# A fused retention and feed-forward kernel: one unit more transposed by DMA, half a group more by seven products, and a new order of all instructions

## The chip, the cores and the metric

One core of one Trainium2 chip. Engines: TensorE (PE, matrix products), VectorE (DVE), ScalarE (ACT), GpSimd (POOL, here only an issuer of DMAs) and SyncE (SP, another issuer of DMAs). The metric is device time in microseconds; of several runs the median is used.

## The reference

```python
scores = q @ k^T / sqrt(64)                       # 8 batches, 8 heads, 576 positions, head dim 64
ret    = scores * gamma[h] ** (i - j) for i >= j, else 0
attn   = ret @ v
x      = attn, heads side by side                 # 4608 tokens x 512
h      = x @ w_in                                 # 512 x 2048
out    = max(0.01 h, h) @ w_out                   # 2048 x 512, float32
```

## The kernel before

The tokens are cut into 36 units of 128 (each two chunks of 64) and 9 groups of 512 tokens (four units). A unit `u` goes through these jobs:

- `ld{u}.1`, `.0`, `.2`: load k, q, v (a DMA from SP or POOL; the pool holds four units).
- `ck`, `cq`, `cv`: cast k, scale q and v to half precision (one DVE instruction, or on ACT eight scalings, one for each head, for q and v).
- `tp{u}.1`, `.0` on TensorE and the copies `yt{u}.1`, `.0`: the transposed k and q. From unit `CFG["turned"]` on, one DMA transpose `tr{u}` on SP's queue does that instead.
- `sb` (state sums, TensorE), `st`, `sg` (running state, DVE), `sx` (its cast).
- `ca` (the state's part of the output and the scores, TensorE), `mk` (mask, DVE), `ow` (own chunk's part, TensorE), `x{u}` (the result into `xT`).

Layer one of group 0 and group 1 is plain: jobs `h{g}.{f}.{t}` of 8 or 16 products on TensorE, followed by the activation `l...` on ACT (L643). The groups from 2 on take layer one by a scheme of seven products for four quadrants (Strassen's in Winograd's form): `a{g}.{n}.p1` to `.p7`, four matmuls of 256 columns each, on sums of inputs `xs` (DVE) and of weights `ws` (DVE), with copies `cA`, `u2`, `k5` out of the accumulators and the sums `12` and `22` on DVE. Layer two of each group is done the same way: `b{g}.p1` to `.p7`, each in two parts of eight matmuls, with input mixes `m` and weight mixes `wm` on DVE. `wi{f}` loads a quarter of `w_in` (two DMAs of POOL that convert to half precision), `wo{c}` a quarter of `w_out`, `so` stores.

A word `+7@0` is seven matmuls on a tile of zeros into accumulator 0, whose result nobody reads (`filler`, L957).

The order of all jobs is written out by hand as a list of words, `ORDER`, and each engine runs its own jobs in that order, one after the other; `@n` names the accumulator a job takes. The table `ENGINE` says which of DVE and ACT does a job that either can do. A job that waits holds up every later one on its engine.

## Time and profile before

| | |
|---|---|
| time, median of 3 runs | 283.44 us (283.22 to 283.71) |
| the profiled execution's own time | 285.72 us |
| its span | 283.9 us |
| PE busy | 273.8 us (96%) |
| DVE, ACT busy | 237.9 us (84%), 198.2 us (70%) |
| mean granted clock of TensorE | 0.982 |

Times in the profile are those of one execution, counted from the start of its span. A busy TensorE is not one at its peak, since its records overlap; so the length of a row of products, or the time from one job to the next, says what a product costs. The time that is idle on an engine counts only where the chain that ended last runs through it.

### The profile page before, as it was taken

The numbers are of one execution on the slowest core, as the hardware profiler recorded it, in microseconds if no ns is written. First come the engines' busy times: TensorE is split into PE (matmuls) and PEld (weight loads), VectorE is DVE, ScalarE is ACT, GpSimd is POOL, SyncE is SP. The second block draws the span as 40 slices with busy tenths as digits, with TensorE's granted clock in tenths as the row PEclk, the third lists the DMA queues.
The fourth block names the chain that finished last, engine by engine and source line by source line (L and its number), as shares of the span: only waits on it lengthen the run. The fifth ranks groups of instructions, "written<-read, shape, count | busy, mean of one in ns | idle before, by whom it ended". The sixth has DMA issues, their size and how long they took to land.

```text
span 283.9 us, 10247 instructions
## 1 busy us (share of the span) xinstructions
PE 273.8 (96%) x4411; PEld 232.3 (82%) x4411; DVE 237.9 (84%) x453; ACT 198.2 (70%) x434; POOL 40.9 (14%) x54
## 2 busy tenths in 40 slices
PE   7759999999999999999999999999999999999994
PEld 3539888888888888888888888888888888888883
DVE  2964568999998999889999999998899998975851
ACT  2233687676767997699859877898598975815840
POOL 8957795300000000000000000000000000000000
PEclk9956999999999999999999999999999999999999
DMA  7999999987898884699959479999499062002103
GB/s 224 274 195 213 220 262 249 299 204 177 235 178 196 198 215 95 171 225 231 194 130 251 91 208 186 239 171 242 106 248 210 6 183 76 3 2 105 45 18 130
DMA packets 114062, 49.00 MB, mean 173 GB/s; under 512 B 102689, under 2 KB 107425, under 8 KB 114017
## 3 DMA queue, kind: packets, MB, share of 16 engines
q1 hardware_dynamic: 106592, 34.87, 53.8%
q0 software_dynamic: 7136, 13.37, 19.7%
q8 instruction: 34, 0.56, 0.8%
q10 hardware_dynamic: 288, 0.11, 0.1%
q14 instruction: 12, 0.09, 0.1%
HBM read 36.81 MB, written 9.44 MB: 163 GB/s over the span
## 4 chain that ended last, share of the span: by engine, by line
PE 92%; DMA 4%; POOL 2%; DVE 1%; issue 0%; POOLq 0%
PE acc L898 40%; PE acc L822 31%; PE acc L636 11%; PE ot L540 5%; DMA t<-in_v_dram 4%; PE sc L443 2%; PE sc L434 2%; POOL t L344 2%; PE acc L400 1%; PE acc L957 0%; DVE osb L935 0%; DVE v L366 0%; DVE s L449 0%; POOLq L344 0%; POOLq L1009 0%
## 5 line engine op out<-in xcount | busy, mean ns | idle before, releaser
L898 PEld LDWEIGHTS <-gt 128*128 128x128 f16 x720 | 69.0, 98 | 8.7 <-issue 0.2
L898 PE MATMUL acc<-w_out,gt 128*128 128x256 f16 x432 | 54.4, 273 | 0.0
L822 PEld LDWEIGHTS <-w_in 128*128 128x128 f16 x448 | 43.1, 98 | 5.7 <-issue 0.3
L840 ACT ACTIVATE gt<-acc 128x512 f16<-128x512 f32 x56 | 33.4, 599 | 10.8 <-PE acc L822 10.6
L898 PE MATMUL acc<-w_mix,gt 128*128 128x256 f16 x288 | 36.2, 273 | 0.0
L822 PEld LDWEIGHTS <-w_sum 128*128 128x128 f16 x336 | 32.3, 98 | 4.2
L848 ACT ACTIVATE gt<-sum 128x512 f16<-128x512 f32 x56 | 33.9, 632 | 2.2 <-DVE sum L844 2.1
L822 PE MATMUL acc<-xT,w_in 128*128 128x256 f16 x224 | 33.1, 273 | 0.0
L822 PE MATMUL acc<-xs,w_sum 128*128 128x256 f16 x224 | 32.8, 273 | 0.0
L822 PE MATMUL acc<-xs,w_in 128*128 128x256 f16 x224 | 32.5, 273 | 0.0
L636 PE MATMUL acc<-xT,w_in 128*128 128x256 f16 (+1 forms) x320 | 32.2, 262 | 0.0
L449 DVE TENSOR_TENSOR s<-sc,cs 128x512 f16<-128x512 f32 x36 | 24.7, 686 | 8.3 <-PE sc L434 7.6
L898 PEld LDWEIGHTS <-mix 128*128 128x128 f16 x288 | 27.7, 98 | 3.3
L636 PEld LDWEIGHTS <-w_in 128*128 128x128 f16 x320 | 27.1, 104 | 2.5 <-DVE xT L589 0.2
L761 ACT COPY acc<-acc 128x512 f32<-128x512 f32 x32 | 18.4, 574 | 13.3 <-PE acc L822 9.1
L643 ACT ACTIVATE gt<-acc 128x512 f16<-128x512 f32 x32 | 17.9, 600 | 12.2 <-PE acc L636 12.1
L844 DVE TENSOR_TENSOR sum<-acc,u 128x512 f32<-128x512 f32 x28 | 19.1, 687 | 3.3 <-PE acc L822 1.9
L772 ACT COPY u<-acc 128x512 f32<-128x512 f32 x26 | 15.3, 589 | 8.9 <-PE acc L898 4.5
L366 DVE TENSOR_TENSOR qk<-t,cs 128x512 f16<-128x512 f32 x29 | 19.8, 685 | 1.9 <-DMA t<-in_q_dram 1.9
L844 DVE TENSOR_TENSOR sum<-acc,k 128x512 f32<-128x512 f32 x28 | 19.2, 686 | 2.3 <-PE acc L822 2.0
L366 DVE TENSOR_TENSOR v<-t,cs 128x512 f16<-128x512 f32 x29 | 19.7, 685 | 1.6 <-DMA t<-in_v_dram 1.5
L589 ACT CAST xT<-ot 128x512 f16<-128x512 f32 x28 | 16.3, 588 | 6.7 <-PE ot L540 6.4
(64 smaller groups left out, 453.8 us busy)
## 6 DMA issues: line engine op xcount, KB each, us to landing
out_dram<-osb SPq DMA_DIRECT2D x17, 512.0 KB, 4.3
t<-in_k_dram SPq DMA_DIRECT2D x22, 256.0 KB, 3.9
t<-in_q_dram SPq DMA_DIRECT2D x22, 256.0 KB, 3.8
t<-in_v_dram SPq DMA_DIRECT2D x20, 256.0 KB, 4.3
t<-in_v_dram POOLq DMA_DIRECT2D x12, 256.0 KB, 7.2
t<-in_q_dram POOLq DMA_DIRECT2D x10, 256.0 KB, 7.6
t<-in_k_dram POOLq DMA_DIRECT2D x10, 256.0 KB, 6.8
w_in<-in_moe_w_in_dram POOLq DMA_DIRECT2D x8, 256.0 KB, 7.8
```

The costliest lines, as they stand in the source:

```text
L366: engine[e].tensor_tensor(out=out, in0=t32[u, 2 * x][:], in1=decay(u, x), op=MUL)
L449: landed[u] = nc.vector.tensor_tensor(out=s[:], in0=sc[:, :, 0], in1=mask_sb.unsqueeze(1).unsqueeze(1).to_broadcast([P, 2, NP, CH]), op=MUL,)
L589: copies[xe](out=x_of(u).rearrange("q c (j t) -> q j c t", j=2), in_=at)
L636: nc.tensor.matmul(out=a[:, n, :], lhsT=w_in16[:, c, (f0 + n) * P : (f0 + n + 1) * P], rhs=x[:, c, t0 : t0 + nt], start=(n == 0 and c == 0 ...
L643: nc.scalar.activation(out=y[:, f0 : f0 + nf, t0 : t0 + nt], in_=a[:], func=mybir.ActivationFunctionType.Lrelu)
L761: copies[ce](out=B[:], in_=A[:])
L772: op("u2", ue, lambda: copies[ue](out=u2[:], in_=B[:]), [done["6"]], [u2], [B])
L822: nc.tensor.matmul(out=r[:, f, :], lhsT=w[:, c, (2 * n + f) * P : (2 * n + f + 1) * P], rhs=rhs[:, c, :], start=fresh and c == 0 and f == ...
L840: w = op(what, "ACT", lambda: nc.scalar.activation(out=to(), in_=r[:], func=lr), after, [y], [r])
L844: what, "DVE", lambda: nc.vector.tensor_tensor(out=s[:], in0=r[:], in1=plus[:], op=ADD),
L848: f"l{g}.{n}.{what}", "ACT", lambda: nc.scalar.activation(out=to(), in_=s[:], func=lr), [j], [y],
L898: nc.tensor.matmul(out=(r[tb] if isinstance(r, tuple) else r)[:, tb, :], lhsT=lhs[n]()[:, f, tb * P : (tb + 1) * P], rhs=rhs[n][:, f, :], ...
```

## The change

Three settings change and all orders are made anew:

- `turned` from 12 to 11: unit 11 is transposed by DMA (`tr11`) and not on TensorE (`tp11`, `yt11`).
- `half` from 0 to 1: in group 1, the plain jobs of half of the hidden columns (`h1.4`, `h1.6`, `h1.12`, `h1.14`) are replaced by two sets of seven products, `a1.2` and `a1.3`, with their sums of inputs `xs1`.
- `ORDER` and `ENGINE` are another list: there are 39 zero matmuls in place of 27, in lots of 13, 2, 4, 6, 7, 3, 1 and 3 ahead of the first layer-one job.

The helper for loading `w_in` can also load eighths now, which is unused (`halved` is empty).

```diff
-    turned=12,
-    half=0,
+    turned=11,
+    half=1,
+    halved=(),
...
 ORDER = """
-    ld0.1 ld0.0 ld1.0 ld0.2 ld1.1 ld1.2 ck0 +6@0 +1@1 +1@2 tp0.1@3 ld2.1 yt0.1 ld2.0 cq1 cq0 +7@0 tp1.0@1 ld3.1 yt1.0
...
+    ld0.1 ld0.0 ld1.0 ld1.1 ld0.2 ld1.2 ld2.2 ld2.1 cq0 cq1 ck0 ld3.2 +13@0 +2@1 tp0.0@2 ck1 tp0.1@3 ld2.0 cv0 yt0.1
...
+    tp3.0@3 ck3 sx2 cv3 +1@1 tp3.1@2 yt3.0 yt2.0 sb3 x0 cq4 ca2 tp4.0@1 st3.0 mk2 ld5.2 yt3.1 +3@3 ow2 st3.1 ld5.1
+    h0.0.0@0 sg3.1 x2 ck4 ld5.0 h0.0.128@3 sx3 yt4.0 ca3 l0.0.128 tp4.1@2 mk3 h0.0.256@1 wi2 ld6.1 h0.4.256@3
...
-        w_in_job[f] = add(f"wi{f}", "POOL", run)
+        j = add(f"wi{f}" + ("" if i is None else "ab"[i]), "POOL", run)
+        for e in (0, 1) if i is None else (i,):
+            w_in_job[2 * f + e] = j
...
-                after = [w_in_job[0], w_in_job[1], w_in_job[2], w_in_job[3]]
+                after = list(dict.fromkeys(w_in_job[f] for f in range(8)))
```

The engines' rows at three places. First POOL's DMA queue from its tenth load on, before (the names end with the tensor loaded; `x2` are two halves):

```order
L344 DMA t_1_216<-in_k_dram 64x8x64 x2
L344 DMA t_2_250<-in_v_dram 128x8x64
L612 DMA w_in_113<-in_moe_w_in_dram 64x4x512 x4
L344 DMA t_0_350<-in_q_dram 64x8x64 x2
L344 DMA t_2_363<-in_v_dram 64x8x64 x2
L612 DMA w_in_113<-in_moe_w_in_dram 64x4x512 x2
```

and after the change:

```order
L346 DMA t_0_229<-in_q_dram 64x8x64 x2
L346 DMA t_1_270<-in_k_dram 128x8x64
L614 DMA w_in_113<-in_moe_w_in_dram 64x4x512 x2
L346 DMA t_1_314<-in_k_dram 64x8x64 x2
L614 DMA w_in_113<-in_moe_w_in_dram 64x4x512 x2
L346 DMA t_2_426<-in_v_dram 64x8x64 x2
```

The two rows ahead of the weights were unit 4's k and unit 3's v (`t_2_250`); now they are unit 4's q and unit 3's k (`t_1_270`), and two transfers of weights follow in place of four.

Second, DVE in the opening around the loads of unit 3, before: `v_372` is unit 3's v (`cv3`), `s_403` and `s_472` are the masked scores of units 1 and 2 (`mk1`, `mk2`), `s_505` the state of unit 3.

```order
L477 TENSOR_TENSOR s_346<-sc,s_346 128x256
L407 COPY qkT<-acc 128x512 x2
L366 TENSOR_TENSOR v_372<-t_2_250,cs 128x512
L449 TENSOR_TENSOR s_403<-sc,cs 128x512
L449 TENSOR_TENSOR s_472<-sc,cs 128x512
L407 COPY qkT<-acc 128x512
L477 TENSOR_TENSOR s_505<-sc,s_346 128x256
```

and after: `qk_424` is unit 3's q and k (`cq3`, `ck3`), `v_445` its v (`cv3`), the copy of `qkT` is `yt2.0`, `qk_474` is `cq4`, `s_392` and `s_507` are `mk1` and `mk2`.

```order
L451 TENSOR_TENSOR s_392<-sc,cs 128x512
L479 TENSOR_TENSOR s_394<-sc,s_279 128x256
L368 TENSOR_TENSOR qk_424<-t_0_190,cs 128x512
L479 TENSOR_TENSOR s_394<-sc,s_394 128x256
L364 CAST qk_424<-t_1_270 128x512
L368 TENSOR_TENSOR v_445<-t_2_154,cs 128x512
L409 COPY qkT<-acc 128x512
L368 TENSOR_TENSOR qk_474<-t_0_229,cs 128x512
L479 TENSOR_TENSOR s_505<-sc,s_394 128x256
L451 TENSOR_TENSOR s_507<-sc,cs 128x512
```

The mask of unit 1 stood behind the scaling of unit 3's v; now it stands ahead of unit 3's loads, and the mask of unit 2 stands behind the cast of unit 3's k.

Third, DVE where the new seven-product sets of group 1 begin; before there are none, and this is the row of after (`xs` are the sums of inputs, `w_sum` and `w_in` those of weights, `mix` and `gt` group 0's mixes):

```order
L715 TENSOR_TENSOR w_in_113<-w_in_113 128x2x512
L878 TENSOR_TENSOR mix<-gt 128x1024
L715 TENSOR_TENSOR w_sum<-w_in_113 128x2x512
L806 TENSOR_TENSOR xs<-xT 128x512
L715 TENSOR_TENSOR w_sum<-w_in_113,w_sum 128x2x512
L806 TENSOR_TENSOR xs<-xT 128x512
L479 TENSOR_TENSOR stmp<-sc,s_1120 128x256
L806 TENSOR_TENSOR xs<-xT,xs 128x512
```

Four sums of inputs, and the sums of weights of their half, now stand ahead of the mixes that layer two of group 0 needs.

## The prediction

> **What bounds the kernel now.** I read the page first (busy time by engine, TensorE in 40 slices), then the windows, then TensorE's waits. In a window row the columns are length, busy time of PE, weight loads, DVE, ACT and POOL with their counts, granted clock, DMA share, GB/s.

> ```profile
> PE 273.8 (96%) x4411; PEld 232.3 (82%) x4411; DVE 237.9 (84%) x453; ACT 198.2 (70%) x434; POOL 40.9 (14%) x54
> PE   7759999999999999999999999999999999999994
> 22.00:284.00 262.00, 258.03 (x4152) 223.55 (x4148) 224.78 (x424) 191.57 (x423) 23.95 (x28) 0.99 0.73 168
> PE acc L400 <- DVE qkT L407: 2.2, 1, 2.2
> PE ot L540 <- DVE s L449: 1.1, 1, 1.1
> ```

> By slices TensorE is full from the fourth on and idle for 0.6 of the last one, 4.2 us, the store after the last product. It is busy 258.0 of the last 262 us, so that tail is all that is missing: its waits (total, times, longest) lie in the opening. The time is when TensorE's gapless stream starts, plus the work in that stream, plus what is lost to half clock.

> The opening by windows of 3.4 us, TensorE alone, then its chain and its stream (start, duration; in brackets the idle time before):

> ```profile
> 12.20:15.60 3.40, 1.60 (x48) 0.99 0.98 177
> 15.60:19.00 3.40, 2.02 (x33) 0.50 1.09 169
> 19.00:22.40 3.40, 2.88 (x95) 0.50 1.11 253
> 22.40:25.80 3.40, 3.40 (x35) 0.51 1.02 202
> 25.80:29.20 3.40, 3.40 (x79) 1.00 0.78 199
> 10.62 7.53 DMA t<-in_v_dram
> 18.17 0.69 DVE v L366
> 21.95 4.66 PE L636 MATMUL acc<-xT,w_in 128*128 128x128 f16 x48
> 27.05 1.96 PE L636 MATMUL acc<-xT,w_in 128*128 128x128 f16 x32
> ```

> The clock halves at 15.6, behind a window with 1.60 us of work in 3.40, and comes back at 25.8, behind a full one. The chain through the opening is POOL's twelfth load, unit 3's v: issued at 10.62, landed at 18.15. The layer-one stream starts at 21.95. At half clock it makes a matmul in 97 ns (4.66/48), later in 61 (1.96/32); by 25.8 it has made 40 of them (3.85/0.097).

> **The change, part by part.** *Half of group 1 by seven products.* Eight plain jobs of 8 matmuls go, fourteen of 4 come: 64 becomes 56.

> ```profile
> 58.37 0.87 PE acc L636 x8
> 46.06 0.98 PE acc L636 x8
> 117.22 1.31 PE acc L822 x12
> 29.25 0.33 PE acc L400 x4
> 47.03 0.22 PE acc L400 x4
> ```

> A matmul of 256 columns takes 109 ns in both kinds (0.87/8, 1.31/12), so eight less are -0.87 us. Where a job follows another kind it took 0.98, 0.11 more; six jobs more could cost 6 x 0.11 = 0.66, which leaves -0.2. I take -0.87: the products stand between others of 256 columns. *Unit 11 by DMA.* Two transposing jobs go, 0.44 to 0.66 us; I take 0.5, and nothing for the DMA: unit 11's scores stand behind more than a product of layer two (16 matmuls of 109 ns) after it is issued; if it came late, the loads' wait below would show it first. On SP's queue the loads of units 13 to 15 stand behind its wait for the casts of unit 11; those of before wait there as long for buffers. Together -1.4 us (-0.6 to -1.6).

> *The opening.* Twelve zero matmuls more (39 for 27), and other loads first. POOL's first twelve issues are as long and as many as before; unit 3's k is now the twelfth, then the first quarter of w_in. Of DVE's rows I add the longest ACT run ahead of them: the scalings of unit 1's q, unit 1's v and unit 2's v go to ACT.

> ```profile
> 6.35 1.30 DVE L366 TENSOR_TENSOR qk<-t,cs 128x512 f16<-128x512 f32 x2 [1.93 <-DMA t<-in_q_dram]
> L370 ACT ACTIVATE v<-t,cs 128x64 f16<-128x64 f32 x56 | 14.1, 342 | 0.0
> 16.55 0.58 ACT L407 COPY qkT<-acc 128x512 f16<-128x512 f16 x1
> 10.61 0.42 DVE L362 CAST qk<-t 128x512 f16<-128x512 f32 x1
> 10.95 0.68 DVE L366 TENSOR_TENSOR qk<-t,cs 128x512 f16<-128x512 f32 x1
> 14.05 0.68 DVE L366 TENSOR_TENSOR qk<-t,cs 128x512 f16<-128x512 f32 x1
> 14.65 0.42 DVE L477 TENSOR_TENSOR s<-sc,s 128x256 f32<-128x256 f32 x1
> 14.36 0.62 ACT L362 CAST qk<-t 128x512 f16<-128x512 f32 x1 [2.49 <-DMA t<-in_k_dram]
> 19.40 0.63 POOL L612 DMA_DIRECT2D w_in<-in_moe_w_in_dram  x1 [0.29 <-DMA w_in<-in_moe_w_in_dram]
> 20.65 0.62 POOL L612 DMA_DIRECT2D w_in<-in_moe_w_in_dram  x1 [0.62 <-DMA w_in<-in_moe_w_in_dram]
> ```

> Steps follow each other on DVE after 0.34 us (half rows, casts) or 0.60 (whole rows). Unit 1's q lands at 6.35; eight scalings on ACT take 2.0 us (14.1/7); three lots, the second from unit 1's v at about 8.6, end at 12.6. A copy and a cast (0.5 each) end at 13.6, unit 1's scores at about 14.1, their mask at 14.7; a sum, a scaling and a sum (0.34, 0.60, 0.34) bring DVE to ck3, the cast of unit 3's k, at 16.0. The zero matmuls up to there stand in the waits that ACT's lots make; I cost them at nothing. If a whole lot of seven outlasted its wait, 1.7 us (0.24 each) would come on top. At ck3 DVE waits for the twelfth load, and with it cv3, unit 2's transposed copy and mk2, which are queued behind it; TensorE, with one zero matmul in that place, waits at tp3.1. If the load lands as before, at 18.15, TensorE has some 0.7 us of work between 15.6 and 19.0. A window with 1.60 lost the clock, so this one does too, at 19.0 instead of 15.6.

> ```profile
> 17.36 0.61 PE L400 MATMUL acc<-ident,qk 128*128 128x128 f16 x4
> 19.82 0.45 PE L443 MATMUL sc<-v,qk 64*64 64x64 f16 x16
> 20.14 0.45 PE L434 MATMUL sc<-qkT 64*64 64x64 f16 x16
> 20.52 1.04 PE L957 MATMUL acc<-idle 128*128 128x512 f16 x2
> 8.89 1.68 PE L957 MATMUL acc<-idle 128*128 128x512 f16 x7
> 21.48 0.43 PE L540 MATMUL ot<-s,v 64*64 64x64 f16 x16
> ```

> From 18.15 at half clock: ck3 to 18.5, cv3 to 19.1, sb3 (0.45) to 19.6, ca2 (0.11 and 0.45) to 20.15, a transpose to 20.6. DVE is done with mk2 at 21.0 (after cv3: 0.34, 0.60, 0.34, 0.60), but three zero matmuls stand ahead of its reader, 0.52 us each (1.04/2): to 22.15. ow2 ends at 22.6, and there layer one starts; its weights have landed (20.65). To 25.8 it makes 33 matmuls, 7 fewer than now: 7 x 0.061 = +0.4 us.

> *Sum.* +0.4 - 1.4 = -1.0 us. The profiled execution took 285.72 us (span 283.9), 2.3 above the median; the same difference on the median of 283.44 gives **282.4**. About 0.2%, 0.57 us, is what a measurement here tells from no change.

> *DVE and ACT behind the opening.* The set adds to DVE four sums of inputs (0.42), four sums of products (0.69) and two copies of a1.3 (0.69), less one copy of unit 11 (0.42).

> ```profile
> 30.00:80.00 50.00, 49.96 (x855) 43.28 (x853) 42.72 (x84) 37.36 (x94) 17.05 (x20) 1.00 0.99 238
> 60.00:100.00 40.00, 40.00 (x669) 34.94 (x667) 37.96 (x74) 31.15 (x82) 0.00 (x0) 1.00 0.85 195
> L802 DVE TENSOR_TENSOR xs<-xT 128x512 f16<-128x512 f16 x14 | 5.8, 420 | 0.3 <-ACT xT L589 0.3
> L844 DVE TENSOR_TENSOR sum<-acc,u 128x512 f32<-128x512 f32 x28 | 19.1, 687 | 3.3 <-PE acc L822 1.9 <-ACT u L772 1.0
> L775 DVE COPY k<-acc 128x512 f32<-128x512 f32 x14 | 9.6, 689 | 3.2 <-PE acc L822 2.5 <-PE acc L898 0.6
> ```

> That is 1.7 + 2.8 + 1.4 - 0.4 = 5.4 us on 42.7 in the 50 us from 30 to 80. I cost it at nothing: from 60 to 100 DVE is already busy 38.0 of 40 us, and TensorE 40.0. Without that cover it costs up to what the next rival says.

> **The rivals.** *The load lands in its turn.* Load eleven landed at 14.36; at the same pace the twelfth is there before DVE asks at 16.0. Then TensorE never waits long, the clock stays, and the second w_in transfer (20.65) starts layer one: 5.15 us at 61 ns are 84 matmuls for 40, -2.7, with -1.4: **279.3**. For: the twelfth came 3.8 us after the eleventh, which may be chance. Against: the same bytes go the same way, with w_in right behind.

> *The load is late, but the clock stays.* Layer one starts at 21.3, with 74 matmuls by 25.8: -2.1 - 1.4, **279.9**. The row against it: the longest wait before was 2.2 us, and the clock fell. [...]

> *DVE becomes the bound* (the slower side). Between 30 and 80 it has 7.3 us idle, 5.4 are taken. If the in-order waits that made those 7.3 remain, DVE ends the stretch up to 5.4 us late, and TensorE waits for sums and copies; 4.7 of the idle time lies before 40, where little stood in its queue. Half, 2.7, gives -1.0 + 2.7: **285.1**. It decides from 1.6 us of such waits. Against it stand the 60 to 100 row and ACT's 37 of 50.

> *The saving is eaten* by job switches (0.66) or a second lost window at 25.8: about **283.3**, no change.

> **How the numbers follow.** Forecast 0.46; load in turn 0.18; clock stays 0.08; DVE bound 0.20; eaten 0.08. Faster: 0.36 of the first, whose own range (281.8 to 283.2, by the bounds of the -1.4 term) reaches into 0.2%, with 0.18 and 0.08: 0.62. Same: 0.10 of the first and half of the eaten, 0.14. Slower: the DVE case and the other half, 0.24. The range leaves out half of the earliest case and half of the DVE case: 279.6 to 285.0.

> **What would show it.** Right: DVE's longest early wait is at the cast of unit 3's k, until about 18; half clock from 19.0 to 25.8; layer one from 22.6; no TensorE wait after 30. Wrong: that cast runs at 16 and the clock row shows no 5 (279); TensorE waits for DVE's L848, L779 or L806 between 35 and 80 (285).

## The result, and the profile after

The changed kernel takes **286.4 us** (median of 19 runs, 284.04 to 287.75); the kernel before, on the same chip, 283.2 (19 runs, 282.67 to 285.04). The ratio is 1.0088 with a 95% interval of 1.0068 to 1.0108: **slower by 0.9%**, where 282.4 and a gain were forecast. Here and below the median and the range are of all runs of a kernel; its ratio leaves out a run more than 1.5% above the kernel's fastest.

The traced execution is one of the shorter ones: 284.4 us, span 282.6. Its page:

```profile
span 282.6 us, 10307 instructions
PE 271.2 (96%) x4407; PEld 229.1 (81%) x4407; DVE 241.7 (86%) x462; ACT 207.0 (73%) x479; POOL 41.4 (15%) x54
PE   8889699999999999999999999999999999999993
PEclk9999999999999999999999999999999999999998
```

The clock row has no 5: nothing was lost to half clock. TensorE has a 6 in its fifth slice (28 to 35 us), where before it was full. The opening by the same windows as before (length, busy PE, weight loads, DVE, ACT and POOL with counts, granted clock, DMA share, GB/s):

```profile
12.20:15.60 3.40, 3.14 (x94) 1.68 (x92) 3.17 (x8) 1.14 (x3) 3.40 (x7) 1.00 0.92 165
15.60:19.00 3.40, 2.55 (x70) 1.79 (x60) 3.14 (x8) 2.18 (x4) 2.22 (x4) 1.00 1.13 213
19.00:22.40 3.40, 3.24 (x86) 2.66 (x85) 2.38 (x7) 2.10 (x4) 2.78 (x5) 1.00 1.18 267
22.40:25.80 3.40, 3.36 (x97) 3.00 (x96) 2.04 (x5) 1.45 (x4) 3.04 (x5) 1.00 0.96 222
25.80:29.20 3.40, 1.83 (x54) 1.62 (x52) 2.58 (x6) 1.46 (x3) 2.58 (x4) 1.00 1.15 247
29.20:32.60 3.40, 2.31 (x45) 2.24 (x45) 0.00 (x0) 0.69 (x2) 2.66 (x4) 1.00 1.13 230
```

From 12 to 25.8 TensorE is much busier than before and keeps its clock. Then come two windows, worked 1.83 and 2.31, that were full before. The timeline of DVE at the cast on which the forecast turned, and of TensorE (start, duration, in brackets the idle time before the row and what ended it):

```profile
16.43 0.42 DVE L364 CAST qk<-t 128x512 f16<-128x512 f32 x1
18.74 0.81 PE L961 MATMUL acc<-idle 128*128 128x512 f16 x3
20.03 1.96 PE L640 MATMUL acc<-xT,w_in 128*128 128x128 f16 x32
27.37 0.26 PE L542 MATMUL ot<-s,v 64*64 64x64 f16 x11
30.29 0.23 PE L542 MATMUL ot<-s,v 64*64 64x64 f16 x5 [2.66 <-issue]
```

The cast of unit 3's k has no bracket: DVE came to it at 16.43 and did not wait; the twelfth load had landed. Layer one starts at 20.03, not at 22.6. But at 27.63 TensorE stops for 2.66 us in the middle of a job, after 11 of 16 products on tiles that were ready for all 16. The releaser is `issue`: the engine waited for nothing that the profile shows. TensorE's four largest waits (total, times, longest):

```profile
PE ot L542 <- issue: 2.7, 1, 2.7
PE acc L961 <- DVE idle L314: 1.2, 1, 1.2
PE sc L445 <- DVE v L368: 0.9, 2, 0.7
PE acc L402 <- ACT gt L647: 0.5, 1, 0.5
```

The first is new and is the largest; the second is the start of the kernel, which before has too. Without the first, and all else the same, the span would be 279.9.

### The profile page after: what moved, and what is told of

The parts are those of the page before. It is cut to its first block, busy times and chain, and to the rows that moved or that the text cites. A ratio compares the mean times of both kernels' runs of the same rounds, so it can differ in the third digit from the quotient of the medians.

```text
span 282.6 us, 10307 instructions
## 1 busy us (share of the span) xinstructions
PE 271.2 (96%) x4407; PEld 229.1 (81%) x4407; DVE 241.7 (86%) x462; ACT 207.0 (73%) x479; POOL 41.4 (15%) x54
## 3 DMA queue, kind: packets, MB, share of 16 engines
q0 software_dynamic: 7136, 13.37, 19.6%
## 4 chain that ended last, share of the span: by engine, by line
PE 90%; DVE 3%; DMA 2%; issue 1%; ACT 1%; POOL 1%; POOLq 0%
PE acc L902 40%; PE acc L826 33%; PE acc L640 8%; PE ot L542 5%; PE sc L445 2%; PE sc L436 2%; DMA t<-in_v_dram 2%; PE acc L402 1%; DVE s L451 1%; POOL t L346 1%; DVE s L479 1%; DVE qk L368 0%; DVE qkT L409 0%; ACT gt L647 0%; DVE v L368 0%
## 5 line engine op out<-in xcount | busy, mean ns | idle before, releaser
L826 PEld LDWEIGHTS <-w_in 128*128 128x128 f16 x480 | 46.0, 98 | 6.2 <-issue 0.4
L844 ACT ACTIVATE gt<-acc 128x512 f16<-128x512 f32 x60 | 35.5, 601 | 11.8 <-PE acc L826 11.2
L826 PEld LDWEIGHTS <-w_sum 128*128 128x128 f16 x360 | 34.5, 98 | 4.7
L826 PE MATMUL acc<-xT,w_in 128*128 128x256 f16 x240 | 35.7, 273 | 0.0
L826 PE MATMUL acc<-xs,w_sum 128*128 128x256 f16 x240 | 35.3, 272 | 0.0
L826 PE MATMUL acc<-xs,w_in 128*128 128x256 f16 x240 | 35.0, 273 | 0.0
L848 DVE TENSOR_TENSOR sum<-acc,u 128x512 f32<-128x512 f32 x30 | 20.6, 687 | 5.7 <-PE acc L826 4.9
L640 PE MATMUL acc<-xT,w_in 128*128 128x128 f16 (+1 forms) x256 | 23.8, 246 | 0.1
L848 DVE TENSOR_TENSOR sum<-acc,k 128x512 f32<-128x512 f32 x30 | 20.4, 686 | 3.0 <-ACT k L779 2.5
L372 ACT ACTIVATE v<-t,cs 128x64 f16<-128x64 f32 x88 | 22.1, 343 | 0.6 <-DMA t<-in_v_dram 0.6
L776 ACT COPY u<-acc 128x512 f32<-128x512 f32 x25 | 14.7, 587 | 10.3 <-PE acc L902 5.2
L640 PEld LDWEIGHTS <-w_in 128*128 128x128 f16 x256 | 19.2, 98 | 1.9 <-issue 0.4
L765 ACT COPY acc<-acc 128x512 f32<-128x512 f32 x29 | 16.7, 575 | 5.1 <-PE acc L826 3.9
L372 ACT ACTIVATE qk<-t,cs 128x64 f16<-128x64 f32 x72 | 18.2, 339 | 2.9 <-DMA t<-in_q_dram 2.6
```

The lines of the kernel that those rows point to most:

```text
L372: nc.scalar.mul(out=out[:, h, :], in_=t32[u, 2 * x][:, h, :], mul=tab_sb[:, w, x, h : h + 1])
L640: nc.tensor.matmul(out=a[:, n, :], lhsT=w_in16[:, c, (f0 + n) * P : (f0 + n + 1) * P], rhs=x[:, c, t0 : t0 + nt], start=(n == 0 and c == 0 ...
L765: copies[ce](out=B[:], in_=A[:])
L776: op("u2", ue, lambda: copies[ue](out=u2[:], in_=B[:]), [done["6"]], [u2], [B])
L826: nc.tensor.matmul(out=r[:, f, :], lhsT=w[:, c, (2 * n + f) * P : (2 * n + f + 1) * P], rhs=rhs[:, c, :], start=fresh and c == 0 and f == ...
L844: w = op(what, "ACT", lambda: nc.scalar.activation(out=to(), in_=r[:], func=lr), after, [y], [r])
```

## The experiments

**Theory.** TensorE ran out of instructions. Each matmul here comes with a weight load (4407 of each), so 128 matmuls are 256 instructions. The page has a queue of its own for instructions:

```profile
q8 instruction: 34, 0.56, 0.8%
```

34 packets of 16 KB; if all are TensorE's, its 8,814 instructions (4407 and 4407) make 259 to a packet. In the trace of the changed kernel the queue starts no packet from 21.3 to 27.6 us (the first line below), and one from 27.7 to 30.3 (the other two), while POOL's loads (q0) fill the DMA engines:

```profile
q0 software_dynamic: 803, 1.47, 104.0%
q0 software_dynamic: 286, 0.71, 104.0%
q8 instruction: 1, 0.02, 2.2%
```

By the theory TensorE, quicker than before through the opening, came to the end of such a block before the next one was there. **Rivals:** the wait is a dependency that the profile does not name; or the new order of the opening is at fault whatever its count; or DVE, or the two new sets of products, cost the time.

**The kernel before again.** No edit.

> The kernel before, unchanged, to see the granted clock and the span of many executions. Theory (the profiled execution of before, 285.72 us with a clock of 0.982, was not typical): most executions show a clock of 0.99 or more and a span near 281.4 us, so that half clock costs before almost nothing in its median. Rival (0.982 is typical and profiling adds the 2.3 us): clocks near 0.982 in most executions, spans near 283.9.

283.2 us (282.68 to 284.88, 12 runs), ratio 0.9999 (0.9982 to 1.0017). The traced execution has a span of 281.3. Two of its windows, and below them its layer-one rows from TensorE's timeline:

```profile
14.95:18.35 3.40, 1.72 (x86) 1.34 (x89) 2.80 (x6) 1.16 (x3) 2.04 (x4) 0.99 1.05 148
18.35:21.75 3.40, 3.40 (x73) 2.44 (x62) 2.78 (x7) 0.58 (x1) 1.39 (x3) 0.51 1.17 257
```

```profile
20.09 2.71 PE L636 MATMUL acc<-xT,w_in 128*128 128x128 f16 x32
23.07 1.05 PE L636 MATMUL acc<-xT,w_in 128*128 128x128 f16 x16 [0.27 <-ACT xT L589]
24.38 1.96 PE L636 MATMUL acc<-xT,w_in 128*128 128x128 f16 x32
```

One window of half clock, not three, and layer one from 20.09, not 21.95. The mean clock of its 12 runs is 0.987 to 0.994; the execution on which the forecast was built had 0.982. It was not typical.

**Most zero matmuls taken out.** The words `+4` to `+3` behind the first two lots go (24 matmuls and 24 weight loads).

```diff
-    ld3.0 +4@0 sb0 cv1 ... cv2 +6@0 sb1 ... sx1 +7@1 ow0 ... st2.0 +3@2 ow1 ... cv3 +1@1 tp3.1@2 ... yt3.1 +3@3 ow2
+    ld3.0 sb0 cv1 ... cv2 sb1 ... sx1 ow0 ... st2.0 ow1 ... cv3 tp3.1@2 ... yt3.1 ow2
```

> After the change, without the 24 zero matmuls behind the first 15 (48 TensorE instructions fewer ahead of the 2.7 us wait at 27.6). Theory F (TensorE runs out of instructions there, since 16 KB blocks of 256 come only every 6.6 us under POOL's loads): the wait moves back by 48 instructions, layer one is 24 matmuls further when it comes, and it is shorter by about 1 us; about 0.5 to 1.5 us faster than the change. Rival C (the clock decides, the zeros keep it up): the clock halves from about 19 in most executions and the time rises by 2 to 3 us.

287.96 us (286.2 to 290.86, 4 runs; 287.25 without the run of 290.86), ratio 1.0139 (1.0102 to 1.0176), clock 0.976. Slower than the change, where theory F expected a gain: with the zeros the clock was 1.00 in the changed kernel's windows above, as rival C has it. Without them it is half from 12.7 to 26.4 us, as in these of its windows,

```profile
15.60:19.00 3.40, 2.56 (x52) 1.91 (x52) 3.40 (x8) 2.15 (x4) 1.78 (x3) 0.50 1.08 199
22.40:25.80 3.40, 3.40 (x53) 3.14 (x51) 0.17 (x2) 1.16 (x3) 2.66 (x4) 0.50 0.98 220
```

and the wait is still there, shorter, in another job and 4 us later, by TensorE's timeline:

```profile
30.99 1.01 PE L639 MATMUL acc<-xT,w_in 128*128 128x128 f16 x15
33.37 1.11 PE L639 MATMUL acc<-xT,w_in 128*128 128x128 f16 x17 [1.37 <-issue]
```

Again TensorE had issued 478 matmuls, which without the 24 zeros is a later place in the program.

**Each zero matmul as four of 128 columns.** The same columns, 234 instructions more.

```diff
-            nc.tensor.matmul(out=a[:, 0, :], lhsT=idle[:, 0:P], rhs=idle, start=True, stop=True)
+            for i in range(4):
+                nc.tensor.matmul(
+                    out=a[:, 0, i * P : (i + 1) * P], lhsT=idle[:, 0:P], rhs=idle[:, i * P : (i + 1) * P], ...
```

> After the change, every zero matmul of 512 columns made as four of 128: the same time on TensorE, 234 instructions more. Theory F: the stock of instructions is used up earlier, at about 21 to 24 us, waits there and at 28 sum up to 2.7 us plus about 3 to 5 us, and the time rises by 2 to 4 us. Rival C: TensorE is as busy as before, so clock and time stay within 0.5 us.

286.66 us (286.21 to 288.96, 4 runs), ratio 1.013 (1.0095 to 1.0166). The wait has moved to a whole block earlier and a whole block later: after 351 matmuls (0.95 us) and after 606 (0.51). In size theory F missed: the two waits make 1.5 us, not 5.7 to 7.7, and the time is only 0.3 us (by the ratios 1.2) above the change's, with half clock from 19.6 to 26.5 us in the trace.

**Fewer instructions for the same work.** Group 0's first eight columns of layer one, made as eight jobs of 128 tokens, become eight of 256 tokens: the same multiplications in 64 matmuls and 64 weight loads fewer, all between 20 and 34 us.

```diff
-    for u in range(4):
-        for fb in range(2):
-            ...
-                layer1(0, 4 * fb + i, 2 if fb in CFG["halved"] else 4, u * P, P)
-    for i in range(8):
-        layer1(0, HF + 2 * (i % 4), 2, 2 * P * (i // 4), 2 * P)
+    for i in range(16):
+        layer1(0, 2 * (i % 8), 2, 2 * P * (i // 8), 2 * P)
```

> After the change, the eight layer-one jobs of group 0 that work on 128 tokens (16 matmuls of 128 columns) made as eight on 256 tokens (8 matmuls of 256 columns): the same products, 128 TensorE instructions fewer between 20 and 34 us. Theory F: the wait of 2.7 us at 27.6 goes or falls under 1 us, and the time falls by 1.5 to 3 us. Rival (the wait comes from a transfer or a semaphore at that place): it stays, and the time stays within 0.5 us.

**283.04 us** (281.76 to 284.04, 10 runs), ratio 0.9983 (0.9961 to 1.0004), where the change has 1.0088. No wait by `issue` is left, and the time fell by 3.4 us (by the ratios 3.0), where 1.5 to 3 were expected. By 30 us this kernel had come to 453 matmuls (first count of the window), and the changed one to 478 already when its wait began:

```profile
0.00:30.00 30.00, 26.01 (x453) 16.35 (x454) 19.71 (x42) 17.21 (x44) 25.95 (x37) 1.00 0.98 241
```

```profile
0.00:29.00 29.00, 24.10 (x478) 15.66 (x479) 19.09 (x42) 15.70 (x41) 24.97 (x36) 1.00 0.99 237
```

It comes to the 478th only at 32.5, later than the 30.29 at which the changed one went on. The rival would have it that 256-token jobs are quicker in themselves. Their row in this kernel says that they hardly are:

```profile
20.03 1.92 PE L639 MATMUL acc<-xT,w_in 128*128 128x256 f16 x16
```

The same products took 1.96 us as 32 narrow matmuls; there are four such lots, so the jobs themselves give some 0.2 us of the 3.4 (an estimate from these two rows). The control is **the same rewriting in the kernel before**, where two jobs had to move behind `x3`:

```diff
-    h0.4.128@1 ... h0.4.0@0 ... h0.4.256@3 ... h0.0.256@1 ... h0.0.128@2 ... h0.0.0@3 ... x3 ... h0.4.384@2 h0.0.384@1
+    h0.4.0@1 ... h0.6.0@0 ... h0.0.0@3 ... h0.2.0@1 ... x3 h0.4.256@2 ... h0.6.256@3 h0.0.256@1 ... h0.2.256@2
```

> The control: the kernel before, with the same rewriting of group 0's eight 128-token jobs as eight of 256 tokens; two of them have to move behind the last transposition of the half. The kernel before has no wait for instructions there, so by the theory there is nothing to gain: 283.0 to 285.0 (0 to 2 us dearer for work moved behind unit 3's copy), ratio 1.000 to 1.006. Rival (the wide jobs are faster in themselves): 3.4 us less, 280.0, ratio 0.988.

285.85 us (284.48 to 287.63, 6 runs), ratio 1.0091 (1.0057 to 1.0125): no gain, and dearer than either theory had it, with a new wait of 0.9 us for unit 3's copy and, in the traced execution, half clock from 16.3 to 23.1 us and from 29.9 to 33.3. The new order costs something of its own here, so the control shows only that the rewriting does not gain 3.4 us wherever it is made; the size of its own effect is better read from the two rows above.

**Half the dose.** Only the jobs of the first 256 tokens are widened, 64 instructions fewer.

```diff
+    for i in range(4):
+        layer1(0, 2 * i, 2, 0, 2 * P)
-    for u in range(4):
+    for u in range(2, 4):
```

> In the changed kernel only the four 128-token jobs of group 0's first 256 tokens (columns 0 to 7) become four jobs of 256 tokens: 32 matmuls and 32 weight loads fewer, ahead of the place of the wait. Half the dose of the kernel that had 64 and 64 fewer. Theory (instructions run out at a block border): the border, 961 instructions in, lies 64 instructions later in the program, which is about 2 us of work; the wait of 2.7 us shrinks to 0.3 to 1.2 us, still with no releaser, and the time is 283.0 to 284.5. Rival (the wide jobs are faster in themselves, or it was the order): half of the 3.4 us, 284.7, with the wait either whole or gone. Rival (any narrowing of the gap below some length keeps the clock, and the wait itself is cheap): wait of 1 to 2 us and a time at 282 to 283.

285.62 us (283.37 to 287.87, 10 runs), ratio 1.0069 (1.0034 to 1.0104), above the 283.0 to 284.5 expected. The wait at the old place fell to 0.46 us as the theory has it, but the time fell by less than 1 us: in the traced execution two more waits by `issue` came, of 0.66 and 1.45 us. The windows up to inside each wait, where the first count is of matmuls:

```profile
0.00:29.60 29.60, 26.25 (x478) 16.63 (x479) 19.17 (x42) 16.30 (x42) 26.30 (x37) 1.00 0.98 243
0.00:38.20 38.20, 33.44 (x605) 22.35 (x606) 23.92 (x53) 21.36 (x52) 33.30 (x45) 1.00 1.01 247
0.00:210.00 210.00, 204.29 (x3549) 169.27 (x3550) 188.73 (x368) 168.53 (x407) 41.22 (x54) 1.00 0.97 212
```

**The wait provoked where there was none.** The kernel before with its 27 zero matmuls split in four, 162 instructions more; the edit is the one shown above.

> The wait provoked where there was none: the kernel before, with each of its 27 zero matmuls of 512 columns as four of 128 (the same columns, 81 matmuls and 81 weight loads more, all ahead of layer one, which otherwise stays as it was). Theory (TensorE gets its instructions in blocks of 256, one in some 6.5 us while the loads run): at the place where before had issued some 757 instructions it now has to have 919, close to the border at 961: one or more waits without a releaser, 0.5 to 3 us together, between 17 and 34 us, at multiples of 256 instructions (705 or 961), and 284.0 to 287.0. Rival (the wait belongs to the new order of the changed kernel, not to the count of instructions): no wait without a releaser over 0.3 us and 283.0 to 283.8.

285.74 us (284.84 to 286.47, 6 runs), ratio 1.0079 (1.005 to 1.0107). The wait appears in the kernel before, inside a layer-one job:

```profile
20.71 0.93 PE L636 MATMUL acc<-xT,w_in 128*128 128x128 f16 x7
23.21 3.71 PE L636 MATMUL acc<-xT,w_in 128*128 128x128 f16 x41 [1.57 <-issue]
```

Its trace has 10.2 us of half clock too, but two runs with a clock of 0.993 and 0.994, as in before, took 285.2 and 284.8 us, still above before's median of 283.5.

All waits by `issue` of over 0.15 us between 15 and 50 us, and three later ones, with the matmuls that TensorE had issued by then:

| kernel | matmuls issued | wait, us |
|---|---|---|
| the change, five traces | 478 each | 2.66, 1.61, 1.18, 2.52, 1.75 |
| the same, one of them also | 1373 | 0.42 |
| the same, another also | 351 | 0.27 |
| few zeros | 478, 3549 | 1.37, 0.46 |
| zeros split | 351, 606 | 0.95, 0.51 |
| half the dose | 478, 605, 3549 | 0.46, 0.66, 1.45 |
| before, zeros split | 351 | 1.57 |
| the wide kernel with one job moved (below) | 350 | 0.17 |

351, 478, 605 are 127 apart; 1373 is 6 x 128 behind 605, and 3549 another 17 x 128. Jobs, lines, times and kernels differ, the distance is in each of these 16 waits, to within a matmul, a multiple of 127 or 128 matmuls. No dependency of the program lies so: the wait is read here as one **for instructions**. The packets of the instruction queue fit that. In the change's trace one starts at 27.85 us and lasts 0.91, and TensorE goes on at 30.29, 1.5 us behind its end; its packets of the first 50 us start 6.1 to 7.5 us apart. In the second of the traces below, too, the queue starts none from 21.7 to 26.8 us and one from 26.8 to 29.4, and TensorE goes on at 29.37.

**More traces of the changed kernel.** Of its 19 runs, 8 had a mean clock of 0.996 or more and a median of 284.4; 11 had 0.988 to 0.994 and a median of 287.1. Four more traced executions (no edit) show where the second kind loses its clock.

> The changed kernel unaltered, for a trace of one more of its executions. Theory (TensorE runs out of instructions near 27.6 us): the same wait for nothing that the profile shows, 2 to 3 us, after the 478th matmul again (within one or two), and layer one from 20.0. If the execution takes about 287, its trace also shows a stretch of 3 to 7 us at half clock that begins within 4 us behind that wait, and no other wait of TensorE above 1 us that the execution of 286.4 lacks. Rival (the slow executions lose their time somewhere else, in the opening or on DVE): no half clock behind the wait, or a half-clock stretch that begins before 27.

> The changed kernel unaltered, one more traced execution, because about half of its executions take 286 to 288 with a mean granted clock of 0.988 to 0.994 and none of these has a trace yet. Theory: in such an execution the wait without a releaser near 27.6 us is 3 us or longer and a stretch of 3.4 us at half clock follows within 4 us behind it; in one of 284 to 285 the wait is under 2.8 us and the clock stays at 0.996 or more. Rival: the half clock lies in the opening before 20 us, or at the end, and the waits are the same in both.

> As for the look before this one: a trace of an execution of 286 to 288 shows a longer wait without a releaser near 27.6 us and a stretch of half clock right behind it (theory), or half clock elsewhere (rival).

> As for the two looks before: in an execution of 286 to 288 a longer wait near 27.6 us with half clock behind it (theory), or half clock elsewhere (rival).

The first (six runs, median 284.88, ratio 1.0071, 1.0033 to 1.0109) and the second (283.49) had full clock, with waits of 1.61 and 1.18. The third (285.92, wait 2.52) and the fourth (286.37, wait 1.75) lost a window. The third's windows:

```profile
24.95:28.35 3.40, 3.33 (x120) 2.97 (x118) 2.23 (x5) 2.09 (x4) 2.98 (x4) 1.00 1.12 215
28.35:31.75 3.40, 0.94 (x22) 0.90 (x22) 0.53 (x2) 0.00 (x0) 2.17 (x3) 1.00 1.09 242
31.75:35.15 3.40, 3.14 (x32) 2.91 (x29) 0.00 (x0) 1.82 (x4) 2.30 (x4) 0.52 1.15 259
```

and the fourth's:

```profile
27.60:31.00 3.40, 1.65 (x57) 1.39 (x54) 1.49 (x4) 0.52 (x2) 3.19 (x5) 1.00 1.02 271
31.00:34.40 3.40, 3.14 (x32) 2.98 (x30) 0.00 (x0) 1.36 (x3) 3.06 (x4) 0.50 1.15 212
```

The lost clock lies right behind the wait, as expected. That it takes a wait of 3 us or more was wrong: 1.75 us cost the window and 2.66 did not. What the lost windows have in common is the one before them: TensorE busy for 0.94 and 1.65 of 3.4 us here, 1.72 in the kernel before above. In the fourth the whole wait of 1.75 us (28.51 to 30.26) falls into that one window, in the third nearly all of the 2.52 (28.29 to 30.81). The change's own trace, which kept the clock, can be set beside them. In the trace of before the clock is recorded as full for 10.24 us from 5.29 on, then half for 10.24, then full again for 259.41: 3, 3 and 76 times 3.413 us. In the change's it is recorded as full from 4.71 us to 281.19, behind the last product, 81 times 3.413. Counted so, its windows around the wait are these:

```profile
25.19:28.61 3.42, 2.44 (x75) 2.19 (x73) 2.93 (x6) 2.07 (x4) 2.75 (x4) 1.00 1.14 218
28.61:32.02 3.41, 1.73 (x36) 1.69 (x36) 0.00 (x0) 0.41 (x1) 2.52 (x3) 1.00 1.10 240
```

The wait of 2.66 us is shared by two windows, and the emptier one, worked 1.73 us, kept the clock where 1.65 lost it. Busy time alone is not the measure, though: with the zeros split in four a window worked 2.24 us (16.23 to 19.64) was followed by half clock. What exactly is counted no run here shows.

**Unit 11 alone.** The kernel before with `turned=11`.

```diff
-tp11.0@2 ... yt11.0 ... tp11.1@2 ... yt11.1
+tr11 (ahead of tr12)
```

> The kernel before with one part of the change alone: unit 11 is transposed by DMA (its eight transposing matmuls and two copies go, one transposing DMA more on SP's queue), everything else in the order of before. Theory (the prediction's term): TensorE saves 0.5 us (eight products and their share of a seam), nothing waits for the transposition: 282.6 to 283.4 where before has 283.4, ratio 0.997 to 1.000. Rival (the transposing DMA arrives late or hinders the loads): a wait of TensorE of over 0.5 us at unit 11's scores and 283.6 to 285.

285.16 us (284.13 to 285.63, 10 runs), ratio 1.0052 (1.0033 to 1.0071): the rival came true, a little above its 285. In the timeline of SP's queue and of TensorE:

```profile
70.99 3.00 SPq L325 DMA_DIRECT2D t<-in_k_dram  x2
74.08 6.08 SPq L367 DMA_TRANSPOSE qkT<-qk  x3
79.59 0.25 PE L521 MATMUL ot<-qkT,st 64*64 64x64 f16 x6 [1.47 <-DMA qkT<-qk]
```

The transposition was issued at 74.08, behind loads on the same queue, and TensorE wanted it at about 78. That is the place that I gave it, not the change's, where it is issued at 64.9 and nobody waits. In its trace the stretch behind the last product is longer too, 4.7 us where before has 3.8. So this run warns of the price of a late DMA; it does not measure by itself the 0.5 us that the transposes save.

**The half of layer one put back.** The wide kernel with `half=0`: eight plain jobs in the places of the two sets, the weight sums that follow from it moved behind them.

```diff
-    half=1,
+    half=0,
...
-a1.2.p1.0 ... a1.2.cA ... a1.2.p5.0 ... a1.2.p3.0 ... (and a1.3, xs1)
+h1.4.0 ... h1.4.256 ... h1.12.0 ... h1.12.256 ... (and h1.6, h1.14)
```

> The changed kernel with the eight wide jobs, and in it the second half of the second group's layer one put back to plain products (eight plain jobs in place of two sets of seven products, 8 matmuls of 512 columns' work more; the three sums of weights that go with it move behind them). It prices this part of the change away from the wait for instructions. Theory (the term of the prediction, 8 matmuls, 0.87 us, with DVE's 5.4 us of sums hidden): 0.9 us dearer than the wide kernel, 283.6 to 284.4, ratio to before 1.001 to 1.004. Rival (DVE's extra sums eat the saving): 282.6 to 283.1, no difference from the wide kernel or better, with DVE's busy time 5 us lower between 30 and 80.

285.34 us (284.75 to 286.23, 6 runs), ratio 1.0071 (1.0046 to 1.0096), some 2.5 us above the wide kernel, with 8 matmuls more. 0.9 was expected; part of the rest are waits that my order of it brought, 0.8 and 0.5 us for DVE among them. The size of the term stays unsettled by this run. The rival, that DVE's sums eat the saving, did not come true in this order: without them DVE had 5 us less to do (237.7 for 242.7) and the kernel was slower. Its 30 us from 50 on, and below it the same stretch with the sets in, from the wide kernel:

```profile
50.00:80.00 30.00, 28.86 (x396) 25.06 (x395) 22.25 (x40) 22.75 (x60) 3.35 (x4) 1.00 0.85 217
```

```profile
50.00:80.00 30.00, 30.00 (x483) 26.18 (x482) 29.41 (x55) 25.51 (x70) 2.91 (x4) 1.00 0.91 227
```

With DVE busy 29.4 of 30 us TensorE does not stand still.

**The wide kernel again, and one job moved in it** to cover a wait of 0.55 us for unit 3's copy:

```diff
-    h0.4.0@1 wi2 ld6.1 h0.6.0@3 l0.4.0 cv4 ld6.0 yt4.1 ow3 sb4 ca4 ld6.2 x3 st4.1 mk4 wi3 h0.0.256@2
+    h0.4.0@1 wi2 ld6.1 l0.4.0 cv4 ld6.0 yt4.1 ow3 sb4 ca4 ld6.2 x3 st4.1 mk4 wi3 h0.6.0@3 h0.0.256@2
```

> The changed kernel with group 0's first eight columns of layer one as eight 256-token jobs, run again on another chip against before. Theory: no wait without a releaser between 20 and 40, granted clock of 0.997 or more, 281.8 to 284.0, ratio to before 0.996 to 1.000. Rival (the first figure was that chip's): 284 to 286.

> The same kernel with one job moved: the fourth wide job (columns 6 and 7 of the first 256 tokens) goes from ahead of unit 3's output products to behind them and behind unit 4's state sums, to cover the 0.55 us in which TensorE waits there for the copy of unit 3's output. Theory: that wait goes, unit 4's state sums wait 0.1 to 0.4 us for the scaled v in its place, and the end comes 0.2 to 0.5 us earlier than with the wide kernel beside it, 281.5 to 283.5. Rival (the wait only moves to the scaled v and to the state behind it): no difference, within 0.2 us of the wide kernel.

Both beat the kernel before, on the same chip: **282.67 us** (281.53 to 283.49, 12 runs), ratio **0.9966** (0.9944 to 0.9987), and 282.58 (281.91 to 285.16, 12 runs), ratio 0.9969 (0.9944 to 0.9995). The moved job took that wait away and brought one of 0.33 for the scaled v and one of 0.17 by `issue`, after 350 matmuls; no difference between the two can be told. With the first wide run (0.9983) the change is worth 0.2 to 0.3% once TensorE is not kept from its instructions, some 0.2 us (0.1%) of it by the wide jobs themselves.

## Why the prediction was wrong, by its own steps

*What bounds the kernel.* Held: TensorE's stream from the start of layer one, plus what is lost to half clock. One source of loss was missing, and this is the step that turned the sign: the stream was taken as gapless, and the supply of the instructions themselves stood at nothing. It cost 1.2 to 2.7 us in one wait.

*The opening (+0.4).* Failed. The twelfth load did not come at 18.15 but in its turn, before 16.43; the first rival described what happened (no 5 in the clock row, layer one at 20.03). Its 279.3 was off because of the next step and the wait for instructions.

*From the profiled execution to the median.* Failed. The sum was made against an execution with 10.2 us of half clock and layer one at 21.95; a typical one has 3.4 us and 20.09. So the better opening was worth 0.06 us in the start of layer one and 0.75 in clock (2.71 for 32 matmuls against 1.96), not the 2.7 of the rival.

*TensorE's work (-1.4).* Held. From the start of layer one to the end of the last product (277.49) the kernel before, in its repeat, takes 257.4 us, 256.4 without the 0.75 of clock and its wait of 0.27. The changed one (278.24) takes 258.2, 254.9 without the wait of 2.66 and the two small ones behind 31 us:

```profile
PE acc L402 <- ACT gt L647: 0.5, 1, 0.5
PE acc L402 <- DVE qk L368: 0.2, 1, 0.2
```

That leaves -1.5. What the prediction did not have is the tail: the last sum on DVE starts right behind the last product in both, before and after,

```profile
277.52 0.69 DVE L935 TENSOR_TENSOR osb<-acc,u 128x512 f32<-128x512 f32 x1 [3.15 <-PE acc L898]
278.28 0.69 DVE L939 TENSOR_TENSOR osb<-acc,u 128x512 f32<-128x512 f32 x1 [1.05 <-PE acc L902]
```

but the span ends 3.8 us behind the product before and 4.4 after, so the store behind it takes 0.6 longer. The other ten traces with this change have 4.4 as well; why, no run shows.

The two waits are all of TensorE's from 31 us on, so *DVE at nothing* held: no wait for its sums or copies, with 3.6 us more of its work (241.7 for 238.1; 5.4 were forecast), and the slower rival, DVE as the bound, did not happen.

*The saving* would have been +0.4 in small waits, -1.5 in work, -0.75 in clock and -0.06 in the start of layer one, with +0.6 in the tail: -1.3 on a typical execution. The wait for instructions took 1.2 to 2.7 back, and in 11 of 19 executions the mean clock is lower by a window or two of half clock, which in the two of this kind that were traced follows the wait. The kernel came out slower by a mechanism that no rival named. The page of before gave a hint: instructions are a row of its queues, and the changed opening puts more matmuls ahead of 28 us without asking when their instructions arrive: 478, where the repeat of the kernel before had come to 418, by its window:

```profile
0.00:28.00 28.00, 22.07 (x418) 14.86 (x419) 17.10 (x38) 10.98 (x19) 22.44 (x33) 0.94 0.96 230
```

*The clock.* The rule used, that a window worked about half is followed by half clock, held in three traces (0.94, 1.65 and 1.72 us), but its border is not sharp: 1.73 us kept the clock in one kernel and 2.24 lost it in another. In the same kernel waits of 1.75 and 2.66 us had opposite outcomes, and the half clock began at different times, about 31.9 us in the third extra trace and 31.0 in the fourth. The rival of a late load under a full clock (279.9) took the clock to stay without a run that shows it; here the load was not late, so these runs did not try it.

*Instructions.* By the table a block is 127 to 128 matmuls with their weight loads, 254 to 256 instructions. No trace has a wait at more than three borders, with 34 or 35 packets of q8 on its page, but one of them cost 1.2 to 2.7 us. In the change's trace TensorE stood still after 957 instructions (478 matmuls and 479 weight loads).

What stays open: why a block comes so late in the opening. While POOL's loads hold the DMA engines at 104% the changed kernel's instruction queue started no packet for 6.6 us. In the traces of before and of the change the first five packets started 1.7 to 6.5 us behind the start of matmuls 97, 224, 351, 478 and 605, in this order (borders counted from the table, every 127 matmuls), none ahead of it; the packet at 27.85 is the third, 4.5 us behind the 351st. No run here took the loads away, so that they are the reason is not shown.

## What to carry to other kernels

Count TensorE's instructions as a resource: here, where a gapless stream of small matmuls ran beside DMA engines at 104%, making the same products in 64 matmuls fewer, and wider ones, was worth more than the order of the jobs (3.4 us, against 1.3 that the change itself would have saved). The waits by `issue` were read as waits for instructions by three signs, which can be looked for elsewhere: they stand in the middle of a job whose inputs are ready, at counts that lie 127 or 128 matmuls or a multiple apart, and in the change's trace 1.5 us lie between the end of a packet of the instruction queue and the end of the wait. And take the baseline of a sum from several executions: their clocks are listed with their times, and one outlier moves every term that hangs on the opening.
